# Attention by pairs of heads: both halves' scores in a row, then both products with v

## The chip, the cores and the metric

The kernel runs on one core of one Trainium2 chip. The metric is the device time of one execution in microseconds (us). PE is TensorE's matmul stream, PEld its weight loads, DVE is VectorE, ACT is ScalarE, SPq the queue in which SyncE issues DMAs.

## The reference, cut to what matters

```python
# hash attention, batch 4, 8 heads, 768 positions, 64 columns a head, all fp32
q_bits = (q @ proj > 0); k_bits = (k @ proj > 0)      # 6 bits a row
mask   = bucket(q_bits)[:, None] == bucket(k_bits)[None, :]
attn   = softmax(where(mask, q @ k.T / 8, -1e9)) ; x = attn @ v
# then an MLP mixer over tokens and over channels (not touched by the change)
```

## The kernel before

Two heads form a pair, and there are 16 pairs. A pair's 768 queries are handled in two halves of 384. For each half PE makes six score chunks. Each is a product of q and k plus a product of the hash bits, which pushes pairs of different buckets far down. ACT exponentiates each chunk into a tile e, DVE adds the six tiles to esd (for the row sums), and PE multiplies them with v. The kernel alternates: scores of one half, then the v product of the half before.

```python
def scores(self):                      # PE sc, ACT e          (first pair's extras cut)
    for c in range(NR):                # NR = 6
        sc = psum.tile([P, 2, 512], F32, name="sc", tag="sc", bufs=3)
        product(sc, qkt, c, True); product(sc, bits, c, False); exponential(sc)
def hashes(n):                         # bits of a later pair
    ps = psum.tile([P, 2, 512], F32, name="hp", tag="sc", bufs=3)[:, 0]
    ...                                # 4 matmuls hp; DVE g = (ps > 0) - 0.5; ACT scales g
    ...                                # 8 DMAs on SyncE, g -> bits
def bounce(pool, n): ...               # 2 DVE transposes, then 4 DMAs to DRAM on SyncE
for n in range(len(pairs)):
    for half in range(2):
        now = Half(n, half); now.scores()
        ...
        now.add(0)                     # three additions (four tiles)
        ...                            # half 0: sums of the pair before, hashes(n + 1), load_qk(n + 2)
        if half and n and n % 2 == 0: bounce(pool, n - 2)
        now.add(1)                     # the other two additions
        weights.turnover() if half else weights.join()   # weight conversion on DVE and ACT
        if before: before.weigh()      # PE acc: v product of the half before
        ...
        if half == 0: load_v(n + 1)
        before = now
```

## Time and profile before

| what | before |
|---|---|
| time, median of 3 runs | 813.13 us |
| span of the profiled run | 811.9 us, PE busy 803.6 |
| attention ends (first token matmul) | 321.75 us |
| one pair of heads on PE | 19.56 us, no idle from 20 us on |
| DVE need of two pairs, one bounce | 37.4 us of 39.12 |

The columns of the chain of waits and of the timeline are start, length, and what ran. A note in brackets at the end of a timeline line is how long the engine sat idle before it, and what ended that idle time. The lines themselves stand in the prediction. There sc is a score chunk, acc a product with v, sums the row sums, hp the product that gives the hash bits.

### The profile page before, as it was taken

What the parts mean: (1) busy time and instruction counts of PE and PEld (TensorE: products, weight loads), DVE (VectorE), ACT (ScalarE), POOL (GpSimd) and SP (SyncE); (2) the same over time, 40 slices, a digit from 0 to 9 for tenths busy, and PEclk for the clock granted to TensorE, in tenths of its full rate; (3) what the DMA queues carried; (4) which work ended last, traced back from release to release, by engine and by line L of the source; (5) the groups of instructions that cost most, each with busy time, mean ns of one, the idle gap of its engine ahead of it and who ended that gap; (6) DMA issues with size and microseconds to landing.
All of it is one profiled execution on the core that took longest, in us unless ns stands there. A gap on an engine that the chain in (4) does not pass through costs nothing.

```text
span 811.9 us, 10567 instructions
## 1 busy us (share of the span) xinstructions
PE 803.6 (99%) x3901; PEld 471.6 (58%) x3901; DVE 664.1 (82%) x869; ACT 423.1 (52%) x675; POOL 42.5 (5%) x69
## 2 busy tenths in 40 slices
PE   9999999999999999999999999999999999999996
PEld 4444444444444444455544448876676886676885
DVE  4889898989898676899575969898669897778985
ACT  5787778788888776111022321236774335775111
POOL 1000000000000000000010110011010012000001
PEclk9999999999999999999999999999999999999999
DMA  4335353547444234562008894499854578730455
GB/s 161 128 137 171 132 174 130 159 133 231 140 130 119 81 81 139 173 214 97 1 0 300 297 349 156 176 274 252 272 136 142 210 231 194 232 118 1 160 178 110
DMA packets 88490, 132.30 MB, mean 163 GB/s; under 512 B 29480, under 2 KB 62704, under 8 KB 86128
## 3 DMA queue, kind: packets, MB, share of 16 engines
q1 hardware_dynamic: 82320, 112.60, 42.4%
q0 software_dynamic: 5552, 18.35, 9.4%
q8 instruction: 33, 0.54, 0.3%
q10 hardware_dynamic: 560, 0.61, 0.2%
q14 instruction: 25, 0.20, 0.1%
HBM read 97.21 MB, written 33.69 MB: 161 GB/s over the span
## 4 chain that ended last, share of the span: by engine, by line
PE 99%; DVE 0%; ACT 0%; issue 0%; ACTq 0%
PE b L709 49%; PE sc L345 20%; PE acc L392 16%; PE t L623 5%; PE t L642 5%; PE sums L416 2%; PE hp L306 1%; PE hw L324 1%; PE idle L454 0%; ACT vt L297 0%; ACT e L352 0%; ACT g L311 0%; DVE second L1128 0%; DVE g L310 0%; DVE bits L326 0%
## 5 line engine op out<-in xcount | busy, mean ns | idle before, releaser
L352 ACT ACTIVATE e<-sc 128x768 f32<-128x768 f32 x192 | 153.1, 811 | 13.4 <-PE sc L345 12.5
L345 PE MATMUL sc<-qk 64*128 64x384 f32 x768 | 158.5, 492 | 0.3 <-ACT e L352 0.3
L709 PE MATMUL b<-R,second 128*128 128x256 f32 (+1 forms) x612 | 150.9, 404 | 0.0
L715 ACT COPY c<-b 128x512 f32<-128x512 f32 (+1 forms) x78 | 37.4, 488 | 187.7 <-PE b L709 174.2
L709 PEld LDWEIGHTS b<-R,second 128*128 128x128 f32 x612 | 116.3, 190 | 31.6 <-issue 17.0
L392 PE MATMUL acc<-e,vn 128*64 128x384 f32 x768 | 130.9, 490 | 0.0
L384 DVE TENSOR_TENSOR esd<-esd,e 128x768 f32<-128x768 f32 x128 | 122.3, 955 | 10.4 <-ACT e L352 0.5
L345 PEld LDWEIGHTS sc<-qk 64*128 64x128 f32 x768 | 66.5, 187 | 55.8 <-issue 45.3
L392 PEld LDWEIGHTS acc<-e,vn 128*64 128x64 f32 x768 | 52.3, 137 | 74.9 <-issue 74.3
L709 PE MATMUL b<-XT,WC 128*128 128x256 f32 (+1 forms) x264 | 82.5, 456 | 0.0
L709 PEld LDWEIGHTS b<-XT,WC 128*128 128x128 f32 x264 | 50.2, 190 | 29.6 <-issue 25.1
L345 PE MATMUL sc<-bits 64*128 64x384 bf16 x384 | 62.9, 323 | 0.2 <-DVE bits L328 0.2
L623 PE MATMUL t<-x,W 128*128 128x512 f32 x96 | 41.8, 593 | 0.0
L642 PE MATMUL t<-W,r 128*128 128x384 f32 x128 | 41.8, 486 | 0.0
L398 ACT ACTIVATE num<-acc,vsum 128x384 f32<-128x384 f32 x32 | 18.6, 581 | 41.6 <-PE acc L392 41.2
L437 ACT COPY rec<-rec 32x384 f32<-32x384 f32 x64 | 32.6, 509 | 12.9 <-DVE rec L431 12.4
L380 DVE SCALAR_TENSOR_TENSOR esd<-e 128x768 f32<-128x768 f32 x32 | 30.5, 954 | 9.3 <-ACT e L352 9.3
L709 PE MATMUL b<-XT,SW 128*128 128x256 f32 (+1 forms) x120 | 34.6, 422 | 0.0
L642 PEld LDWEIGHTS t<-W,r 128*128 128x128 f32 x128 | 24.3, 190 | 17.6 <-issue 1.4
L345 PEld LDWEIGHTS <-bits 64*128 64x128 bf16 x384 | 19.3, 94 | 25.4 <-DVE bits L328 0.8
L709 PE MATMUL b<-TA,WC 128*128 128x512 f32 x72 | 33.8, 592 | 0.0
L709 PE MATMUL b<-TA,SW 128*128 128x512 f32 x72 | 32.9, 592 | 0.0
(176 smaller groups left out, 1052.7 us busy)
## 6 DMA issues: line engine op xcount, KB each, us to landing
second<-left SPq DMA_DIRECT2D x18, 1344.0 KB
raw<-in_moe_w_ch SPq DMA_DIRECT2D x16, 768.0 KB
qk<-in_qk SPq DMA_DIRECT2D x15, 768.0 KB
seen<-in_qk POOLq DMA_DIRECT2D x21, 384.0 KB, 4.2
WC<-hidden_left SPq DMA_DIRECT2D x15, 448.0 KB
vn<-in_v SPq DMA_DIRECT2D x16, 384.0 KB
vt<-in_vT SPq DMA_DIRECT2D x16, 384.0 KB
bounced<-stage SPq DMA_DIRECT2D x32, 192.0 KB
```

The lines of the kernel that those rows point to most:

```text
L345: nc.tensor.matmul(sc[:, i, :HALF], t[rows, 1, P * c : P * c + P], t[rows, 0, qs], start=start, stop=not start,)
L352: nc.scalar.activation(e, sc[:, :, :HALF], ACT.Exp, scale=SCALE)
L380: nc.vector.scalar_tensor_tensor(self.d, es[0], NR * EPS, es[1], op0=ALU.add, op1=ALU.add,)
L384: nc.vector.tensor_tensor(self.d, self.d, e, op=ALU.add)
L392: nc.tensor.matmul(acc[D * i : D * i + D], vn[:, i, c], e[:, i], start=(c == 0), stop=(c == NR - 1),)
L398: nc.scalar.activation(nums[self.n][:, self.half], acc, ACT.Identity, scale=-1.0, bias=vsum,)
L416: nc.tensor.matmul(ps[at : at + 32], ones[:, :32], self.halves[h].d[:, i], start=True, stop=True,)
L437: nc.scalar.copy(rec[other : other + 32, h], rec[at : at + 32, h])
L623: nc.tensor.matmul(ps, W1[:, r, P * j : P * j + P], x[:, r], start=(r == 0), stop=(r == NR - 1),)
L642: nc.tensor.matmul(ps[:, :HALF], r1[:, j, P * cb : P * cb + P], W2[:, j, HALF * half : HALF * half + HALF], start=(j == 0), stop=(j == NJ ...
L709: nc.tensor.matmul(ps, left(k), right(k), start=start and k == ks[0], stop=stop and k == ks[-1], skip_group_check=True,)
L715: nc.scalar.copy(c, ps)
```

## The change

The intent is to run PE's four large blocks of a pair as scores, scores, v, v in place of alternating. Everything else is re-ordered around that: all additions of a half come at once, g of the next pair comes after ten additions, the second v block takes its accumulator from the score ring, and load_v comes after the bounce.

```diff
-            def add(self, k):
+            def add(self):
...
-                for e in (es[2:4], es[4:])[k]:
+                for e in es[2:]:
                     nc.vector.tensor_tensor(self.d, self.d, e, op=ALU.add)
...
+                if self.half:
+                    acc = psum.tile([P, 2, 512], F32, name="acc", tag="sc", bufs=3)[:, 0, :HALF]
...
         for n in range(len(pairs)):
-            for half in range(2):
-                now = Half(n, half)
+            halves = [Half(n, half) for half in range(2)]
+            for now in halves:
                 now.scores()
+                now.add()
+            if before:
+                before.sums()
+            if n + 1 < len(pairs):
+                hashes(n + 1)
+            load_qk(n + 2)
...
+            weights.join()
+            halves[0].weigh()
...
+            weights.turnover()
+            halves[1].weigh()
+            if n and n % 2 == 0:
+                bounce(pool, n - 2)
+            load_v(n + 1)
```

More of the change, by code (lines that the diff above doesn't have):

```diff
@@ L373, in scores @@
                     first_hashes(0, 1)
-            def add(self, k):
+            def add(self):
                 es = self.es
-                if k == 0:
-                    self.d = pool.tile([P, 2, HALF], F32, name="esd", tag="esd", bufs=3)
-                    nc.vector.scalar_tensor_tensor(
-                        self.d, es[0], NR * EPS, es[1], op0=ALU.add, op1=ALU.add,
-                    )
-                for e in (es[2:4], es[4:])[k]:
+                self.d = pool.tile([P, 2, HALF], F32, name="esd", tag="esd", bufs=4)
+                nc.vector.scalar_tensor_tensor(
+                    self.d, es[0], NR * EPS, es[1], op0=ALU.add, op1=ALU.add,
+                )
+                for e in es[2:]:
                     nc.vector.tensor_tensor(self.d, self.d, e, op=ALU.add)
@@ L388, in weigh @@
                 _, vn, _, vsum = loaded[self.n]
-                acc = psum.tile([P, 512], F32, name="acc", tag="acc", bufs=1)[:, :HALF]
+                if self.half:
+                    acc = psum.tile([P, 2, 512], F32, name="acc", tag="sc", bufs=3)[:, 0, :HALF]
+                else:
+                    acc = psum.tile([P, 512], F32, name="acc", tag="acc", bufs=1)[:, :HALF]
                 for c, e in enumerate(self.es):
@@ L460, in attention @@
         )
-        before, both = None, []
+        before = None
         for n in range(len(pairs)):
-            for half in range(2):
-                now = Half(n, half)
+            halves = [Half(n, half) for half in range(2)]
+            for now in halves:
                 now.scores()
-                if half == n == 0:
-                    hashes(1)
-                if half == 0:
-                    add_values(n)
-                now.add(0)
-                quotients = None
-                if len(both) == 2:
-                    quotients, both = Quotients(both), []
-                    quotients.sums()
-                both.append(now)
-                if half == 0 and 0 < n < len(pairs) - 1:
-                    hashes(n + 1)
-                if half == 0:
-                    load_qk(n + 2)
-                if quotients:
-                    quotients.newton()
-                if half and n and n % 2 == 0:
-                    bounce(pool, n - 2)
-                now.add(1)
-                if half:
-                    weights.turnover()
-                else:
-                    weights.join()
-                if before:
-                    before.weigh()
-                if quotients:
-                    quotients.divide()
-                if half == 0:
-                    load_v(n + 1)
-                if half == 0 and n == 2 * NP:
-                    fetch(0, x0)
-                before = now
@@ L498, in attention @@
-        assert not (weights.fetched or weights.begun or weights.ready)
-        quotients = Quotients(both)
-        quotients.sums()
-        quotients.newton()
-        before.weigh()
-        quotients.divide()
+                now.add()
[4 more added lines that the diff above has]
+            load_qk(n + 2)
+            add_values(n)
+            if before:
+                before.newton()
+            weights.join()
@@ new lines, in attention @@
+            halves[0].weigh()
+            if n + 1 == len(pairs):
+                before.divide()
+                before = Quotients(halves)
+                before.sums()
+                before.newton()
+                weights.turnover()
+                halves[1].weigh()
+                break
+            if before:
+                before.divide()
+            weights.turnover()
+            halves[1].weigh()
+            if n and n % 2 == 0:
+                bounce(pool, n - 2)
+            load_v(n + 1)
@@ L506, in careful_attention @@
+            if n == 2 * NP:
+                fetch(0, x0)
+            before = Quotients(halves)
+        assert not (weights.fetched or weights.begun or weights.ready)
+        before.divide()
     def careful_attention(pool, psum):
```

## The prediction

> **What bounds the kernel now.** I read the page's busy row first, then the chain of waits in order of time, then the timeline of one pair, then the groups of one pair with each shape apart. There are 16 pairs, and attention ends near 322 us; what follows is not touched by the diff.
>
> ```profile
> PE 803.6 (99%) x3901; PEld 471.6 (58%) x3901; DVE 664.1 (82%) x869; ACT 423.1 (52%) x675; POOL 42.5 (5%) x69
> ...
> PEclk9999999999999999999999999999999999999999
> ```
>
> TensorE (PE) is busy throughout at full clock, so only less time on it, or a new wait of it, can move the end. A window from 20 to 321.75 us gives 301.75 us of PE busy in 301.75: attention has no gap after its start. One pair in the chain of waits:
>
> ```profile
> 161.01 5.04 PE sc L345 x36
> 166.06 0.78 PE sums L416 x8
> 166.84 0.65 PE hp L306 x8
> 167.49 4.02 PE acc L392 x24
> 171.51 5.05 PE sc L345 x36
> 176.56 4.02 PE acc L392 x24
> 180.58 5.04 PE sc L345 x36
> ```
>
> The columns are start, length, what. A pair is 2 x 5.045 + 0.78 + 0.65 + 2 x 4.02 = 19.56 us, which is also the distance between the starts of two score blocks of one kind (161.01, 180.58). Inside the blocks the timeline shows what a switch between kinds costs:
>
> ```profile
> 171.44 0.92 PE L345 MATMUL sc<-qk 64*128 64x384 f32 x4
> 172.19 0.33 PE L345 MATMUL sc<-bits 64*128 64x384 bf16 x2
> 172.35 0.81 PE L345 MATMUL sc<-qk 64*128 64x384 f32 x4
> 173.00 0.33 PE L345 MATMUL sc<-bits 64*128 64x384 bf16 x2
> ```
>
> The first score chunk after the products with v takes 0.92 us where the next takes 0.81, and starts follow at 0.807 us from then on. Six chunks would be 4.84, the block takes 5.045: 0.20 over. The v block steps by 0.3225 us for each of 12 steps (its weight loads start at 176.86, 177.18, 177.50), that is 3.87, and takes 4.02: 0.15 over.
>
> VectorE (DVE) is the second engine, and it has almost nothing to spare while weights are being converted (pairs 0 to 11):
>
> ```profile
> 70.15 0.55 DVE L310 TENSOR_SCALAR g<-hp 128x384 bf16<-128x384 f32 x1
> 70.89 0.56 DVE L429 TENSOR_TENSOR t<-sums,near 128x384 f32<-128x384 f32 x1 [0.19 <-ACT near L421]
> 71.49 1.03 DVE L431 SCALAR_TENSOR_TENSOR rec<-t,near 128x384 f32<-128x384 f32 x2
> ...
> 78.67 4.15 DVE L384 TENSOR_TENSOR esd<-esd,e 128x768 f32<-128x768 f32 x4
> ```
>
> From one pair of transposes (61.05) to the next (100.17), two pairs of 39.12 us, its idle notes add up to 1.72 us, so it needs 37.4. The four adds of a half depend on each other: 4.15 us for four, one every 1.06.
>
> The last view is the DMA queue, where the hash bits of the next pair leave in eight small transfers:
>
> ```profile
> 169.20 6.13 SPq L316 DMA_DIRECT2D bits<-g  x8
> ```
>
> They are asked for when ScalarE has scaled g (ends 169.17) and are used first at 180.9. Windows of 0.1 us after the same point one pair earlier (149.64) show the first bits moving at 151.0 to 151.2 and later ones every 0.77 us. I estimate 1.8 us from the start of an issue to a usable row.
>
> **What the skill says.** "TensorEngine Tiling (Array Packing)", Key Properties: changing the tiling mode, not just the tile, drains TensorE. The trace agrees in kind: scores are 64*128, v products 128*64, and each change of block shows the 0.15 to 0.20 us above. "VectorE: DVE Perf Modes", on the extra latency of SBUF-source operations, gives (N+151)/0.96 for an fp32 tensor_tensor, 957 ns for 768 columns; the trace has 955. "DMA: Bandwidth & Descriptors", Latency and other measured facts: some 600 ns to the first byte on this kind of queue; the trace has about 0.7 us from the end of an issue (0.70 us long) to the moving bytes.
>
> **The change, part by part.**
>
> *Mode switches.* PE now does scores, scores, sums, hp, v, v: three switches a pair in place of five. One entry into scores (0.20) and one into v (0.15) go: a pair is 12 x 0.807 + 0.20 + 1.43 + 24 x 0.3225 + 0.15 = 19.2 us, 0.36 less. The first pair's blocks are scores, hp, scores, so I count 15: -5.4 us.
>
> *Start.* Scores of half 1 no longer stand behind hp, g and the vt sum on ScalarE. The page's chain had PE starved at 16.8 to 17.4: about -0.6 us.
>
> *Additions in a row.* Let S be the start of a pair's scores, T = S + 9.88 their end. The second exponential ends at S + 2.7 (24.09 and 26.79 in the trace). Ten additions follow without a break, about 10.4 us, so they end at S + 13.1 = T + 3.2. Before, g came after three additions only, 1.5 us after the scores (167.56 against 166.06). Now g stands behind all ten: g ends T + 3.7, its scaling T + 4.3, the eight issues start T + 4.35 and the last at T + 9.8, usable at T + 11.6; the fourth at T + 8.5. PE wants the first four (q and k of half 0) at T + 1.43 + 7.89 + 0.43 = T + 9.75 and the last two (k of half 1) at the fourth chunk, 2.85 us into the scores, T + 12.15. So a regular pair fits with about 0.6 us in hand. The waits of the program before are kept per transfer, so I don't expect PE to wait for all eight at once. The slack was about 4 us before.
>
> *After a bounce.* In a pair with transposes VectorE needs 18.1 (10.3 additions, 2.1 g and Newton, 2.5 join, 0.9 divide, 2.5 end and begin) + 1.76 for them = 19.9 us, over 19.2, and it also waits some 0.4 us for the Square before the conversion's end. It is then about 1.2 us late into the next additions, and the last bits come 0.6 us after they are wanted. Pairs 2, 4, 6, 8, 10 both bounce and convert: 5 x 0.6 = +3 us.
>
> *First pair.* The hash steps of the start hold VectorE till 14.3, so ten additions end near 24.7 while the scores end near 18.8. g is scaled at 25.8, the fourth bits are usable at 29.9 against 27.8 wanted, and the last cost 0.7 more: +2.8 us.
>
> *Other moves.* The second v block's accumulator now sits in the score ring; its buffer is wanted by the third score chunk, 1.6 us after v ends, and ScalarE frees it in 0.7 (0.1 and 0.58): nothing. The fourth esd buffer only takes room. load_v moves behind the bounce: transposes end near T + 13.2, four issues take 3.2 us (62.91), v is asked for at T + 16.5 and should land by T + 19.8, wanted at T + 20.6: nothing, narrowly. Exponentials run at 0.805 against 0.807 of PE: ScalarE keeps up for 12 as for 6.
>
> Sum: 813.1 - 5.4 - 0.6 + 3.0 + 2.8 = 812.9; I take 812.5.
>
> **Rivals.**
> (a) Only the switches count, and the bits and v come in time: 813.1 - 6.0 = 807. For it: every hand-computed margin is within 1 us and could fall well. Against: VectorE at 37.4 of 38.4 us for two pairs.
> (b) The bits become the bound of every pair: if a transfer needs 1 us more than I took, or additions are slower, each of 14 pairs waits 0.5 to 1 us, +7 to +14 over (a)'s 807, plus the first pair's 2.8: 817 to 824. For it: eight issues of 0.77 us in one queue leave only 0.6 us.
> (c) v behind the bounce: if the bounce's small packets hold the queue (one bounce took 7.09 us at 180.28, behind the fetch of x), PE waits 1 to 3 us in seven pairs: 815 to 825.
> (d) PE is starved by exponentials: 0.002 us a chunk between the two rates speaks against it; no loss.
>
> **Range and chances.** The gain is bounded at about 6 us by the switches and the start, which is 0.7%: faster by 2% (below 797) would need something I haven't seen. Slower by 2% (above 829) needs over 1.4 us of waiting a pair, more than (b) and (c) alone give. Range 806 to 819: (a) at its low end, half of (b) at its high end. Faster 0.02, same 0.94, slower 0.04.
>
> **What would show it.** In the chain of waits a pair's blocks should read about 9.9 of scores, 1.4, and 7.9 of acc. If scores and acc are still at 10.1 and 8.04, the switches were not the cause of the 0.35 us. PE idle ended by bits' DMA at the fourth chunk, in pairs 3, 5, 7, 9, 11, and some 2 to 3 us once near 28 us, would confirm the bits; idle before acc ended by vn's DMA would show (c); no PE idle at all, (a). Wrong altogether if waits on VectorE or ScalarE show in PE's scores in every pair.

## The result, and the profile after

The changed kernel takes 816.04 us (median of 4, 815.82 to 816.37) against 813.35 of before in the same session. The ratio is 1.0032, with a 95% interval of 1.0015 to 1.005. A ratio here is the mean time of one kernel's fast runs over the mean of the other's fast runs of the same rounds, so it is not quite the ratio of the medians. Within 2% the two are the same, but the changed kernel is reproducibly slower: two further sessions gave 1.0042 and 1.0048.

The page's busy row of the changed kernel:

```profile
PE 799.3 (98%) x3901; PEld 476.0 (58%) x3901; DVE 664.8 (82%) x869; ACT 427.1 (52%) x675; POOL 42.5 (5%) x69
```

PE is busy 4.3 us less, and yet the span is 2.7 us longer. So PE's own work got cheaper and new idle came in. The chain of waits over pairs 2 and 3 shows both:

```profile
49.32 9.89 PE sc L345 x72
59.21 0.78 PE sums L418 x8
59.99 0.64 PE hp L306 x8
60.64 7.89 PE acc L394 x48
68.53 8.14 PE sc L345 x59
76.67 4.47 DMA vn<-in_v
81.15 0.04 issue
81.19 7.96 PE acc L394 x48
```

See first that a pair without waits is 68.53 - 49.32 = 19.21 us, where before had 19.56. Then, in the next pair, the chain leaves PE at 76.67: it runs through the load of vn, which the v product needed. The table of waits, with the columns total, times and longest, gives all waits of PE for a transfer:

```profile
PE acc L394 <- DMA vn<-in_v: 5.4, 5, 1.3
...
PE sc L345 <- DMA bits<-g: 1.7, 3, 1.1
```

Five waits for vn, each in the pair after a bounce of the conversion stage. The DMA queue shows why. First before, then after, each around the bounce of pair 6:

```profile
136.81 0.36 SPq L288 DMA_DIRECT2D vn<-in_v  x1
137.21 0.43 SPq L290 DMA_DIRECT2D vt<-in_vT  x1
141.15 3.23 SPq L246 DMA_DIRECT2D bounced<-stage  x4
144.48 0.64 SPq L168 DMA_DIRECT2D raw<-in_moe_w_ch  x1
```

```profile
149.35 0.44 SPq L276 DMA_DIRECT2D qk<-in_qk  x1
149.90 0.36 SPq L168 DMA_DIRECT2D raw<-in_moe_w_ch  x1
151.78 4.58 SPq L246 DMA_DIRECT2D bounced<-stage  x4
156.46 0.57 SPq L288 DMA_DIRECT2D vn<-in_v  x1
```

Before, vn was asked for ahead of the bounce, with most of a pair to spare. After, it stands behind four issues that themselves wait for two transposes, and those issues take 4.58 us in place of 3.23, with two loads of 768 KB asked for just before. That these loads are the reason is tested in e4. PE wanted vn at 159.4 and got it at 160.4.

The other wait is in the first pair. The timeline of the changed kernel:

```profile
20.64 4.15 DVE L383 TENSOR_TENSOR esd<-esd,e 128x768 f32<-128x768 f32 x4
24.70 0.55 DVE L310 TENSOR_SCALAR g<-hp 128x384 bf16<-128x384 f32 x1
...
25.99 6.09 SPq L316 DMA_DIRECT2D bits<-g  x8
...
29.65 0.32 PE L345 MATMUL sc<-bits 64*128 64x384 bf16 x1 [1.13 <-DMA bits<-g]
```

The additions keep DVE until 24.7, so g and the eight transfers come late, and PE's first bits matmul of pair 1 waits.

The whole account, from the traces: 15 pairs at 0.35 less are -5.3, and the start is -0.3. The vn waits cost 5.4, plus 0.07 more in each of the five v blocks after them (7.96 against 7.89), together +5.8. Pair 1's scores take 12.3 us from 27.67 to 40.00 in place of 9.89, +2.4. The sum is +2.6. Attention ends at 324.33 us in place of 321.75, which is +2.58, and the rest of the kernel takes the same time in both.

### The profile page after: what moved, and what is told of

Its sections match the earlier page's. It is cut to its first block, busy times and chain, and to the rows that moved or that the text cites. A ratio compares the mean times of both kernels' runs of the same rounds, so it can differ in the third digit from the quotient of the medians.

```text
span 814.6 us, 10602 instructions
## 1 busy us (share of the span) xinstructions
PE 799.3 (98%) x3901; PEld 476.0 (58%) x3901; DVE 664.8 (82%) x869; ACT 427.1 (52%) x675; POOL 42.5 (5%) x69
## 4 chain that ended last, share of the span: by engine, by line
PE 89%; DVE 3%; DMA 3%; ACT 2%; SPq 2%; issue 1%; DVEq 0%; ACTq 0%
PE b L706 49%; PE sc L345 15%; PE acc L394 13%; PE t L620 5%; PE t L639 5%; DMA vn<-in_v 2%; DVE esd L383 1%; SPq L246 1%; ACT e L352 1%; PE sums L418 1%; PE hw L324 1%; PE hp L306 1%; SPq L316 1%; DVE stage L241 0%; ACT rec L439 0%
## 5 line engine op out<-in xcount | busy, mean ns | idle before, releaser
L394 PE MATMUL acc<-e,vn 128*64 128x384 f32 x768 | 127.6, 489 | 5.4 <-DMA vn<-in_v 5.4
L747 POOL TENSOR_TENSOR c<-c 128x512 f32<-128x512 f32 x6 | 8.0, 1339 | 464.2 <-ACT c L712 453.4
```

Of the source, the lines that this page charges most:

```text
L394: nc.tensor.matmul(acc[D * i : D * i + D], vn[:, i, c], e[:, i], start=(c == 0), stop=(c == NR - 1),)
```

## The experiments

Times of different sessions are compared through the ratio to before. Unless said otherwise, before had a median of 813.91 us in the same session.

**e1_v_first: the loads of v ahead of the bounce.**

```diff
             halves[1].weigh()
+            load_v(n + 1)
             if n and n % 2 == 0:
                 bounce(pool, n - 2)
-            load_v(n + 1)
```

> The loads of v and vT are issued before the bounce in place of after it. Theory (v stands behind the bounce in the one DMA queue): the five waits of PE for vn, 5.4 us in the changed kernel's table of waits, go, and 0.07 us of switching after each: 816.0 - 5.7 = 810.3 us. Rival (hash bits after a bounce, as I predicted, hidden behind v's wait so far): vn's waits go but bits take their place in pairs 3, 5, 7, 9 and 11, 0.15 to 0.6 us each: 811 to 813.5 us. No change at all would mean that vn was not what the acc matmuls waited for.

812.17 us, ratio 0.9987 (0.9973 to 1.0). The row for vn is gone from PE's waits; what is left for transfers is:

```profile
PE sc L345 <- DMA bits<-g: 1.9, 4, 1.1
```

The bounce's issues now take 6.4 to 7.6 us in pairs 2 to 10, and nobody waits for them. So vn's place in the queue was the cause of its waits. What the rival foresaw is there too, and the time lies in its range, 1.9 us over the theory's: by the chain, the scores of pairs 4, 8 and 10 are 0.49, 0.03 and 0.36 us longer than 9.89, 0.9 us in all, from bits that come late after a bounce. Another 0.56 us may be the session, in which before was slower by that much. The pairs are not 3, 5, 7, 9 and 11 as expected: the bits that a pair sends out are used by the next one. In pairs 3 and 9 the eight issues of bits also took 6.64 and 6.59 us instead of 6.22, so the late additions need not be the only reason; the two were not separated. In the changed kernel these waits were hidden behind the wait for vn.

**e2_first_hash: pair 1's hashes back between the first pair's halves.**

```diff
             for now in halves:
                 now.scores()
+                if n == 0 and not now.half:
+                    hashes(1)
                 now.add()
...
-            if n + 1 < len(pairs):
+            if n and n + 1 < len(pairs):
                 hashes(n + 1)
```

> Only the hashes of pair 1 go back to between the two score halves of pair 0. Theory (ten additions in front of g cost one wait of about 2.5 us near 28 to 33 us): that wait goes, and 0.3 to 0.5 us at 17 us comes back as in the kernel before: 816.0 - 2.5 + 0.4 = 813.9 us. Rival (the bits are late in every pair, the first only shows it most): under 1 us gained.

816.02 us, ratio 1.0022 (1.0004 to 1.004): a miss, and inconclusive. Its runs lay near 814 (three) and near 817.5 (three), and the profile is of the upper group. There the bits wait is gone, but a first load of q and k came 0.8 us late, the vn waits are 6.3 us, and after the longest of them PE ran slowly. This is the timeline of the weight loads in that v block:

```profile
79.75 0.20 PEld L394 LDWEIGHTS acc<-e,vn 128*64 128x64 f32 x4 [2.80 <-DMA vn<-in_v]
...
81.18 0.24 PEld L394 LDWEIGHTS acc<-e,vn 128*64 128x64 f32 x2 [0.40 <-issue]
81.82 0.24 PEld L394 LDWEIGHTS acc<-e,vn 128*64 128x64 f32 x2 [0.40 <-issue]
...
84.08 0.14 PEld L394 LDWEIGHTS acc<-e,vn 128*64 128x64 f32 x2 [0.18 <-issue]
84.40 0.14 PEld L394 LDWEIGHTS acc<-e,vn 128*64 128x64 f32 x2 [0.18 <-issue]
```

Steps of 0.64 us up to 83.7, then of 0.32: half speed for about 3.2 us (the granted clock from 80.4 to 83.7 was 0.50), and the block took 9.65 us in place of 7.96. The late load, vn waits 0.9 us over the changed kernel's, and the slow block come to 0.8 + 0.9 + 1.7 = 3.4 us, about the distance between the two groups; the other five runs have no profile. It was therefore run again, as e7.

**e3_both: e1 and e2 together.**

> Both edits. Theory (the change is worth 0.36 us of mode switches a pair and lost it to these two waits): 816.0 - 5.7 - 2.1 = 808.2 us, that is 5 us under the kernel before, and PE without idle from 20 us on. Rival (some third loss, e.g. VectorE at its limit, takes over): 811 us or more, with new idle of PE.

809.38 us (809.12 to 809.63), ratio 0.9945 (0.9932 to 0.9958). Of PE's waits for transfers there remains:

```profile
PE sc L345 <- DMA bits<-g: 0.3, 1, 0.3
```

In the window from the first v product (19.69 us) to the token stage (317.05 us) PE is busy 297.0 of 297.36 us. This kernel beats both the one before and the changed one. The expectation was 808.2; by the chain, about 1 us is left in bits after the bounces of pairs 2 and 8 (the next scores but one take 10.5 and 10.3 us).

**e4_fetch_last: only the next raw weights asked for behind v.**

```diff
-            weights.turnover()
+            weights.end()
+            weights.begin()
             halves[1].weigh()
             if n and n % 2 == 0:
                 bounce(pool, n - 2)
             load_v(n + 1)
+            weights.fetch()
```

> Only the fetch of the next raw weights (768 KB) goes behind the load of v; the bounce stays ahead of v. If the bounce's four issues take 4.4 to 5.0 us (3.2 before) because the raw weights ahead fill the queue, they take about 3.3 us again, v lands 1.2 to 2 us earlier, and the waits for vn go or shrink under 0.3 us: 811 to 812 us. If the transposes on VectorE alone set v's time, waits stay near 1.1 us: 815 to 816 us.

812.7 us, ratio 0.9985 (0.9972 to 0.9998). The bounce of pair 6 in the DMA queue, and then PE's waits for vn:

```profile
149.85 2.89 SPq L246 DMA_DIRECT2D bounced<-stage  x4
152.84 0.86 SPq L288 DMA_DIRECT2D vn<-in_v  x1
```

```profile
PE acc L394 <- DMA vn<-in_v: 0.6, 1, 0.6
```

With 768 KB less ahead of them the four issues take 2.8 to 3.4 us in those pairs (4.4 to 5.0 before this edit), and the waits shrink from 5.4 to 0.6 us (0.3 at most was expected), although the transposes come as late as in the changed kernel: the issues of pair 6 start 13.0 us after the end of its scores in both. So the place behind the bounce alone would have been almost free; what made it dear was the load in front of the bounce. It is free only narrowly: after the bounces of pairs 6, 8 and 10 the chain still runs through v. The time is 0.7 us over the expectation; the late bits, which it left out, show here too, as in e1.

**e5a_same_mode, e5b_other_mode, e5c_other_mode_twice: what a change of tile shape costs.** All three are e3_both with one small extra matmul a pair between the two v blocks, into a bank that nobody reads. Its width is 64 in e5a (the shape 128*64 of the v products) and 32 in e5b. e5c adds the same 32-wide one between the two score blocks as well.

```diff
-                    acc = psum.tile([P, 2, 512], F32, name="acc", tag="sc", bufs=3)[:, 0, :HALF]
+                    acc = psum.tile([P, 2, 512], F32, name="acc", tag="sc", bufs=3)
+                    nc.tensor.matmul(acc[:W, 1, :D], ones[:, :W], ones, start=True, stop=True)   # W = 64 or 32
+                    acc = acc[:, 0, :HALF]
...                                                # e5c, in scores(), too
+                    if self.half and c == 0:
+                        nc.tensor.matmul(sc[:32, 0, HALF : HALF + D], ones[:, :32], ones, start=True, stop=True)
```

> e3_both with one small matmul more per pair (64 columns, 128*64 as the v products have, into an unused bank) between the two v blocks. Control for the next two: no switch, only the matmul's own 0.06 to 0.12 us: 809.4 + 16 x 0.1 = 810 to 811.5 us; both theories the same.

> The same small matmul as 128*32, so it makes two switches of tile shape per pair. Theory (a change of shape costs 0.15 to 0.2 us, which is what the change saved): v blocks of a pair grow from 7.89 by 0.3 to 0.5 us in all, 2.5 to 5.5 us over e5a. Rival (the saving came from longer unbroken runs of weight loads, or from what stands between, not from the shape): within 0.8 us of e5a.

> As e5b, and the same again between the two score blocks of a pair: four switches more per pair than e3_both. Theory: the score blocks grow from 9.89 by 0.3 to 0.5 us too, 5 to 11 us over e5a in all, so about the kernel before or worse. Rival: within 1.5 us of e5a.

With 813.88 of before in the session, e5a took 810.94 us (ratio 0.996), e5b 814.41 (1.0007) and e5c 820.57 (1.0081). The chain of waits of e5a, and then of e5b, over one pair's v blocks:

```profile
156.69 4.02 PE acc L396 x24
160.71 0.05 PE acc L390
160.76 3.93 PE acc L396 x24
```

```profile
156.03 4.02 PE acc L396 x24
160.05 0.23 PE acc L390 x2
160.28 4.02 PE acc L396 x24
```

The same matmul costs 8.00 - 7.89 = 0.11 us in the v products' own shape, and 8.27 - 7.89 = 0.38 in another. The two switches are thus 0.27 us a pair, 4.3 us for 16 pairs; the medians differ by 3.5. In e5c the scores of a pair read 5.045 + 0.23 + 5.045 = 10.32 in place of 9.89, 0.43 more, of which 0.32 is left for two switches if the matmul itself costs 0.11 there too. With seven switches a pair, where before had five, e5c's pair is longer than that of before, and so is its time. The rival falls: it is the change of shape that costs, 0.13 to 0.16 us each. The change of the kernel itself saved 0.35 us for two, between 64*128 and 128*64; that pair of shapes was not tested alone, so up to 0.08 us of the 0.35 is not accounted for by e5.

**e6_after_again: the changed kernel unaltered beside e5.**

> The changed kernel unaltered, on the same chip as its neighbours: 816 to 817 us, five waits for vn of 5 to 6.5 us in all. If a wait of PE of about 2 us now and then sends its clock to half for some us, as the profile of e2_first_hash shows once (0.64 us a step at 80.5 to 83.7 after an idle of 2.1), its runs spread or lie in two groups 2 to 3 us apart, while e5a, without such waits, stays within 1 us.

817.45 us (816.56 to 817.89), ratio 1.0042 (1.0028 to 1.0055), with vn waits of 6.2 us, the longest 2.3. That is 0.45 us over the expected range. The runs lie within 1.3 us and not in two groups, and no v block is at half speed in its profile. The control misses as well: e5a's runs lie 2.1 us apart, not within 1, and the profile of its slowest run shows one wait for bits, of 1.8 us, and none for vn. So a wait of over 2 us doesn't always bring the slow spell; what decides it stays open.

**e7_first_hash_again and e8_after_third: e2 and the changed kernel side by side.**

> e2_first_hash once more, beside the changed kernel on the same chip, since its six runs of before lay in two groups (814 and 817.5) and its profile held a late first load (0.8 us), vn waits of 6.3 us and 1.7 us of half clock. Theory: the first wait's 2 us are gained, and only chance waits hid it: 1 to 2.5 us under e8. Rival: v's load waits longer when the first pair is shorter, so nothing is gained while v stands behind the bounce: within 0.7 us of e8.

> The changed kernel unaltered, on the same chip, as the reference for e7: 816 to 817.5 us.

e7 took 814.55 us (ratio 1.0007, 0.9992 to 1.0023) and e8 817.62 (1.0048, 1.0032 to 1.0065); before had 813.61. The first pair's hashes are worth 3.1 us by the medians, with vn waits of 5.7 and 6.2 us in the two profiles. That is more than the 1 to 2.5 us expected, and 0.5 us of it is in the vn waits. The direction of the theory holds, the rival falls, and e2's slower group did not come back; what slowed it is seen only in the one run that was profiled. e1 to e3 gives the same size: 812.17 - 809.38 = 2.8 us.

## Why the prediction was right or wrong

The time lies in the range (806 to 819) and the class holds, but the point of 812.5 was 3.5 us low and on the wrong side of the kernel before: 0.6 us faster was forecast, 2.7 slower measured. Two terms of the sum were wrong in opposite directions, and it is luck that they partly cancelled: 3.0 us that the changed kernel did not pay, and 5.8 that were not foreseen.

- **Mode switches, -5.4.** Right: 15 x 0.35 = 5.3 us, and e5 shows that changes of shape cost nearly as much (0.27 to 0.32 us for two).
- **Start, -0.6.** Right: the first v product comes 0.3 us earlier although this profile's first scores began 0.27 later.
- **Additions in a row.** Right: in pair 6, whose scores end at 138.80, g starts 3.05 us later, and the bits go out at 4.28, as T + 4.35 said. No regular pair waits for bits. The slack of before was misread as about 4 us: reckoned like the 0.6, the last bits were usable at 169.2 + 5.4 + 1.8 = 176.4 and wanted at 180.58 + 2.85 = 183.4, 7 us later.
- **First pair, +2.8.** Right: 2.4 us in the trace, 2.8 to 3.1 by removing it.
- **After a bounce, +3.0.** Mis-sized. (The five parts of VectorE's need add up to 18.3 us, not 18.1.) DVE is 0.8 us late, not 1.2 (g starts 3.86 us after the scores in pair 7, against 3.05), and the changed kernel shows no wait for bits there at all, because vn's wait gave the bits time. Uncovered in e1, the term is 0.9 us, in pairs 4, 8 and 10.
- **"load_v moves behind the bounce ... nothing, narrowly."** This step failed. I put the four issues at the 3.2 us of the trace before, where nothing large was asked for just ahead of them. In the new order q and k of a later pair and the raw weights, 768 KB each, come right before, and the issues took 4.4 to 5.0. In pair 6 v was asked for at T + 17.7 rather than 16.5, then took 3.9 us to land where the sum had 3.3, and PE could start at T + 21.6 rather than at the 20.6 at which it wanted v. The cost was 5.4 us of waiting and 0.4 of longer blocks. e4 shows that this load in front was what mattered. The trace before held a sign of it, which rival (c) quotes: the one bounce with a large fetch right ahead took 7.09 us.

Of the rivals, (c) came true, with smaller waits: 0.7 to 1.3 us in five pairs. The measured time lies in its range of 815 to 825 (its own terms, seven waits of 1 to 3 us over 807, give 814 to 828). After the bounces of pairs 12 and 14, where no more weights are fetched, nothing waits. (In pair 12 the issues, right behind q and k, still took 4.47 us, but with no conversion on DVE they started 11.4 us after the end of the scores and not 13.0.) (a) is what e3 comes close to once both waits are removed: 809.4 against its 807. (b) didn't occur, and exponentials (d) didn't hold PE.

Where did the expected gain go? It is all there on PE, and two transfers gave it back: one that moved behind a bounce, and one whose source now waits for ten additions.

The 957 ns in the prediction is an estimate, from the formula of the page that it names; the 955 ns beside it is the trace's.

## What to carry to other kernels

Grouping matmuls of one tile shape pays per switch removed (here 0.13 to 0.18 us), but re-ordering a loop also re-orders its DMA queue: list each transfer's new neighbours, and put the one with the nearest deadline ahead of the bulky ones. A small operation at the head of a chain of transfers should not be put behind a long run of additions where nothing covers the wait, as in the first round of a loop. When taking a transfer's issue time from a trace, check that what is asked for right ahead of it stays the same.

## What the Trainium skill lacked or had wrong

- "TensorEngine Tiling (Array Packing)", Key Properties, says that a change of tiling mode drains TensorE, and gives no cost. Here two changes cost 0.27 us between 128*64 and 128*32 blocks (e5a, e5b), and by e5c about 0.32 us between 64*128 and 128*32.
- I found no page that gives a time for how long the issuing queue itself is held up by transfers ahead; it would belong to "DMA: Bandwidth & Descriptors". The same four 192 KB issues took 2.9 us (e4), 3.2 (before), 4.6 (after) and 6.4 (e1) in the bounce of pair 6.
- "TensorE: Matmul & The Clock Gate", Part 1, ties half clock to at least one idle window of some 3.4 us. In e2's profile a gap of 2.10 us between matmuls was followed by about 3.2 us at half speed, 1.7 us lost, while waits of up to 2.3 us in e6 left no such trace. The page does say that the window runs free; no run here shows where it lay.
